# Attention's sums and outputs: 128-column weights split into two 64-column halves of the array

## The chip, the core and the metric

One core of a Trainium2 chip runs the whole kernel. The metric is the device time of one execution in microseconds. The engines that matter are TensorE (products into PSUM; the profile gives its products as PE and its weight loads as PEld), VectorE (DVE), ScalarE (ACT), GpSimd (POOL), and SyncE (SP), whose queue issues most transfers.

## The reference, cut to what matters

Four batches, eight heads, 576 positions, 64 columns a head; the attention is linear, without a softmax over positions:

```python
def phi(x):
    proj = np.einsum('bhsd,df->bhsf', x, w_phi)               # 128 features
    proj = proj - np.max(np.abs(proj), axis=-1, keepdims=True)
    return np.concatenate([np.exp(proj), np.exp(-proj)], axis=-1)
q_p, k_p = (phi(q), phi(k))
kv = np.einsum('bhsf,bhsd->bhfd', k_p, v)                     # the sums
z = np.sum(k_p, axis=2)
num = np.einsum('bhsf,bhfd->bhsd', q_p, kv)                   # the outputs
den = np.einsum('bhsf,bhf->bhs', q_p, z)[..., None] + 1e-06
attn = num / den
```

The result, 2304 x 512, goes through two MLPs (512 to 2048 to 512), the first with a leaky ReLU, the second with Mish. The MLP weights arrive as float64, everything else as float32; the result is float32.

## The kernel before, in words

The attention takes the 32 heads in 16 pairs of one batch, one pair a step; `attention(n)` is a step, and it is a software pipeline written out by hand: it loads pair n+3, transposes pair n+2 (`transposes`), projects pair n+1 (`q_proj`, `k_proj`), and makes the sums and outputs of pair n (`kv`, `kv_copy`, `nd`), while `x_t` brings the output of pair n-1 into the MLP's layout. All engines run their instructions in the order in which this code issues them.

Of a head's 576 positions 512 are four blocks of 128 (`NM` = 4); the last 64 (`LEFT`) of the two heads of a pair share a block of 128. For each sign `a` of the exponent, `kv(i, a)` multiplies `kp` as weights (128 positions x 128 features) with `vm` as the moving side: 64 columns of v and 64 columns of ones, so that the sum z comes out beside kv. One more product with `lp` and `vl` (2 x 65 columns) adds the left block. The sums of a pair fill one PSUM bank, `kv_copy` (L415, ACT) copies all 512 columns of it, and `nd` takes 128 columns of `qp` as weights with the 65 columns of `kv` that count, in two calls (c = 0, 1) of 16 profiled products each, c = 1 with the left block's 4 more. A product of two float32 operands appears in the profile as two weight loads and two products. VectorE then divides (L437 to L446).

Projections use operands split into two float32r parts, three products each (`three`, L80 to L82). `q_proj` products are copied by ACT (L389) into `qd`; after each second copy POOL reduces 128 partitions to their largest magnitude (L391), and `q_guard` (L396, DVE) subtracts it. `k_guard` (L351, L352, DVE) does the same for k along the free axis. In even pairs the left block of k of two pairs is projected as well, so such steps have one more pair of DVE instructions; in steps that transpose an even pair there is one more transposition and one more split.

Into the same steps, from step 1 on, the code weaves the conversion of the first MLP's float64 weights (`conv0`: `begin` before the transpositions, `join` between the two `nd` calls). In steps 1 to 10 `join` ends with a VectorE instruction (L149) and a ScalarE copy that waits for it (L202); in steps 11 to 15 the weight is stored by a DMA instead, and L202 is absent. After steps 8 to 11 a `window` splits a slice of the attention's result for the MLP (one more ACT copy and DVE subtraction). The next step's ACT copies of `qd` are queued behind these.

PSUM is used through two rings of four banks: "a" for projections and transpositions, "b" for the sums, the outputs and `x_t`.

Of the kernel before, what the change touches and what calls it, by code (L numbers as in the profile page):

```python
# [10 lines left out]
F32 = mybir.dt.float32  # L11
F32R = mybir.dt.float32r
AF = mybir.ActivationFunctionType
# [10 lines left out]
def attention_two_mlps_kernel(  # L24
# [12 lines left out]
    nc = tc.nc  # L37
    B, H, S, D = q.shape
# [3 lines left out]
    P = 128  # L42
    KD = DM // P
    M = DFF // P
    MAIN = 512
    NM = MAIN // P
    LEFT = S - MAIN
# [4 lines left out]
    HEAD = 2  # L52
    PAIRS = B * NP
    HM = MAIN // 2


    Q_COL = ((HM, 0, HM + P, P), (HM + LEFT, LEFT, HM + LEFT + P, LEFT + P))

# [8 lines left out]
    ap = tc.alloc_tile_pool(name="ap", bufs=2, reuse_waits="tile")  # L67
# [4 lines left out]
    def bank(ring):  # L72
        return ps.tile([P, 512], F32, tag=ring, name=ring)
# [15 lines left out]
    class Conv:  # L89
# [9 lines left out]
        def load(self, ahead):  # L99

            while self.loaded < min(self.at + ahead + 1, len(self.units)):
                u, kind = self.units[self.loaded]
                self.loaded += 1
                if kind == "fetch":
                    continue
                m, x = divmod(u, 2)
                stg = gp.tile([P, DM, 2], I32, tag="stage", name="stage")
                if x == 0:
                    src = w_in[self.which][:, m * P:(m + 1) * P].bitcast(I32).rearrange("(k p) f -> p k f", p=P)
                    dst = stg.rearrange("p (k f) t -> p k (f t)", k=KD)  # L110
                else:
                    src = w_out[self.which][m * P:(m + 1) * P, :].bitcast(I32)
                    dst = stg.rearrange("p f t -> p (f t)")
                nc.sync.dma_start(out=dst, in_=src)
                self.stage[u] = stg
# [122 lines left out]
    with tc.manual_schedule():  # L238
# [8 lines left out]
        nc.vector.memset(two, 2.0)  # L247

        NV = 3
        vmain = [ap.tile([P, 2, NM + 1, D], F32, name=f"vmain{i}", bufs=1) for i in range(NV)]  # L250

        vleft = [ap.tile([P, 2, D + 1], F32, name=f"vleft{i}", bufs=1) for i in range(NV)]
        for i in range(NV):
            nc.vector.memset(vmain[i][:, :, NM, :], 1.0)
            nc.vector.memset(vleft[i], 0.0)
            for r in range(2):
                nc.vector.memset(vleft[i][r * LEFT:(r + 1) * LEFT, r, D:D + 1], 1.0)
# [8 lines left out]
        def load(i):  # L266

            b, p = divmod(i, NP)
            h0 = 2 * p
            s = st[i]  # L270
            for nm, src in (("kn", k), ("qn", q)):
                s[nm] = ap.tile([P, 2, NM, D], F32, tag=nm, name=nm)
                for hs, eng in ([((0, 1), nc.sync), ((1, 2), nc.scalar)] if (i, nm) == (0, "kn") else [((0, 2), nc.sync)]):
                    hs = slice(*hs)
                    eng.dma_start(
                        out=s[nm][:, hs].rearrange("p h t d -> p h (t d)"),
                        in_=src[b, h0:h0 + 2, 0:MAIN, :][hs].rearrange("h (p t) d -> p h (t d)", t=NM),
                    )
                if (i, nm) == (0, "kn"):
                    for r in range(2):  # L280
                        nc.scalar.dma_start(out=wbd[r * D:(r + 1) * D, r, :], in_=w_phi)
            if i % 2 == 0:
                l = lf[i // 2]
                for nm, src, down, along in (("kl", k, 1, 2), ("ql", q, 2, 1)):
                    l[nm] = ap.tile([P, 2, D], F32, tag=nm, name=nm)
                    for r in range(2):
                        g0 = h0 + down * r
                        (nc.scalar if (i, nm) == (0, "ql") else nc.sync).dma_start(
                            out=l[nm][r * LEFT:(r + 1) * LEFT],
                            in_=src[b, g0:g0 + along + 1:along, MAIN:S, :].rearrange("h s d -> s h d"),  # L290
                        )

            def values():
                vm = s["vm"] = vmain[i % NV]
                nc.sync.dma_start(
                    out=vm[:, :, 0:NM, :].rearrange("p h t d -> p h (t d)"),
                    in_=v[b, h0:h0 + 2, 0:MAIN, :].rearrange("h (p t) d -> p h (t d)", t=NM),
                )
                vl = s["vl"] = vleft[i % NV]
                for r in range(2):  # L300
                    nc.sync.dma_start(out=vl[r * LEFT:(r + 1) * LEFT, r, 0:D], in_=v[b, h0 + r, MAIN:S, :])

            return values
# [12 lines left out]
        def transposes(i, *parts):  # L316
# [6 lines left out]
            for nm in parts or "kql":  # L323
                if nm != "l":
                    t = bank("a")
                    for j in range(NM):
                        nc.tensor.transpose(  # L327
                            out=t[:, j * P:(j + 1) * P],
                            in_=s[nm + "n"].rearrange("p h t d -> p (h t d)")[:, j * P:(j + 1) * P], identity=ident)
                    n = HM if nm == "k" else HM + LEFT  # L330
                    hi, lo = (ap.tile([P, 2, n], F32R, tag=f"{nm}t{x}", name=f"{nm}t{x}", bufs=1) for x in "hl")
                    s[nm + "h"], s[nm + "l"] = (x.rearrange("p h n -> p (h n)") for x in (hi, lo))
                    split(hi[:, :, 0:HM], lo[:, :, 0:HM], t.rearrange("p (h n) -> p h n", h=2))
                elif i % 2 == 0:
# [8 lines left out]
        def q_left(i):  # L343
            s, l = st[i], lf[i // 2]
            c = P + (i % 2) * LEFT
            for x in "hl":
                nc.vector.tensor_copy(out=s["q" + x][:, HM:HM + LEFT], in_=l[x][:, c:c + LEFT].bitcast(F32))

# [28 lines left out]
        def q_proj(i, c):  # L377
# [5 lines left out]
            t = bank("a")  # L383
            n = HM + (h == o) * LEFT
            c0 = h * (HM + (1 - o) * LEFT)
            d0 = (1 - o) * (HM + h * LEFT)
# [11 lines left out]
        def kv(i, a):  # L398

            s, l = st[i], lf[i // 2]  # L400
            if a == 0:
                s["kvp"] = bank("b")
            both = s["kvp"].rearrange("p (h a n) -> p h a n", h=2, a=2)

            for h in range(2):
                for t in range(NM):
                    nc.tensor.matmul(out=both[:, h, a, :], lhsT=s["kp"][a][:, h, t, :], rhs=s["vm"][:, h, t:NM + 1:NM - t, :],  # L407
                                     start=(a == 0 and h == 0 and t == 0), stop=False, skip_group_check=True)
            nc.tensor.matmul(out=both[:, :, a, 0:D + 1], lhsT=l["lp"][a][:, i % 2, :], rhs=s["vl"],  # L409
                             start=False, stop=(a == 1), skip_group_check=True)  # L410

        def kv_copy(i):
            s = st[i]
            s["kv"] = ap.tile([P, 4, P], F32, tag="kv", name="kv", bufs=1)
            nc.scalar.activation(out=s["kv"], in_=s["kvp"].rearrange("p (c n) -> p c n", n=P), func=AF.Copy)  # L415

        def nd(i, c):

            s = st[i]
            t = bank("b")  # L420
            ng = 4 + 2 * c
            g = t[:, 0:ng * (D + 1)].rearrange("p (c n) -> p c n", n=D + 1)
            if c == 0:
                s["xn"] = ap.tile([P, NM, 2, D], F32, tag="xn", name="xn")
            for j, u in enumerate(range(2 * c, 2 * c + 2)):
                for h in range(2):
                    for a in range(2):
                        nc.tensor.matmul(out=g[:, 2 * j + h], lhsT=s["qp"][a][:, h, Q_COL[h][u]:Q_COL[h][u] + P],  # L428
                                         rhs=s["kv"][:, 2 * h + a, 0:D + 1], start=(a == 0), stop=(a == 1))
            if c == 1:  # L430

                kv_ = s["kv"].rearrange("p (h a) n -> p h a n", a=2)
                for a in range(2):
                    nc.tensor.matmul(out=g[:, 4:6], lhsT=s["qp"][a].rearrange("p h n -> p (h n)")[:, MAIN:MAIN + P],  # L434
                                     rhs=kv_[:, :, a, 0:D + 1], start=(a == 0), stop=(a == 1))
            den = ap.tile([P, 6], F32, tag="den", name="den")[:, 0:ng]
            nc.vector.tensor_scalar(out=den, in0=g[:, :, D], scalar1=1e-6, scalar2=None, op0=ALU.add)  # L437
            nc.vector.reciprocal(out=den, in_=den)
            nc.vector.tensor_tensor(
                out=s["xn"][:, 2 * c:2 * c + 2].rearrange("p a h d -> p (a h) d"), in0=g[:, 0:4, 0:D],  # L440
                in1=den[:, 0:4].unsqueeze(2).to_broadcast([P, 4, D]), op=ALU.mult)
            if c == 1:
                s["xl"], s["lb"] = xleft[i % 2], t
                for h in range(2):
                    r = slice(h * LEFT, (h + 1) * LEFT)
                    nc.vector.tensor_scalar(out=s["xl"][r, h], in0=g[r, 4 + h, 0:D], scalar1=den[r, 4 + h:5 + h], scalar2=None,  # L446
                                            op0=ALU.mult)

        def x_t(i):
# [45 lines left out]
        def attention(n):  # L495
# [38 lines left out]
            if has_w:  # L534
                nd(w, 0)
# [252 lines left out]
```

## Time and profile before

| | |
|---|---|
| median of 3 runs | 1010.12 us (1010.07 to 1010.75) |
| the profiled execution | 1010.39 us |
| its span, first to last instruction | 1008.4 us |
| PE busy in the span | 1001.2 us, 99% |
| DVE busy, ACT busy | 732.4 us (73%), 500.8 us (50%) |
| `kv` and `nd` on the chain that ended last | L407 6%, L428 6%, L409 1%, L434 1% |

The attention takes about the first 220 us; the MLPs take the rest. The busy shares of the whole span say nothing about one stage, so the views below are cut to the attention's steps. The modelled end of a product's record lies after the start of the next, so the price of a product is read from the distance of starts, or from the chain of work, which counts no time twice.

### The profile page before, as it was taken

What the parts mean: (1) busy time and instruction counts of PE and PEld (TensorE: products, weight loads), DVE (VectorE), ACT (ScalarE), POOL (GpSimd) and SP (SyncE); (2) the same over time, 40 slices, a digit from 0 to 9 for tenths busy, and PEclk for the clock granted to TensorE, in tenths of its full rate; (3) what the DMA queues carried; (4) which work ended last, traced back from release to release, by engine and by line L of the source; (5) the groups of instructions that cost most, each with busy time, mean ns of one, the idle gap of its engine ahead of it and who ended that gap; (6) DMA issues with size and microseconds to landing.
All of it is one profiled execution on the core that took longest, in us unless ns stands there. A gap on an engine that the chain in (4) does not pass through costs nothing.

```text
span 1008.4 us, 14545 instructions
## 1 busy us (share of the span) xinstructions
PE 1001.2 (99%) x5552; PEld 874.8 (87%) x5552; DVE 732.4 (73%) x1366; ACT 500.8 (50%) x840; POOL 68.8 (7%) x36
## 2 busy tenths in 40 slices
PE   9999999999999999999999999999999999999998
PEld 8999999998888889988888888888888988888886
DVE  7788889749984566666435457978977888878875
ACT  6776777635553333333234445545544555445543
POOL 3333333300000000000000000000000000000000
PEclk9999999999999999999999999999999999999999
DMA  6233333224431444444301320000100100001001
GB/s 198 80 113 113 113 104 122 75 75 146 148 104 53 154 138 145 139 146 137 115 1 51 117 94 11 1 1 1 42 0 1 43 1 21 1 0 42 1 1 43
DMA packets 55654, 72.84 MB, mean 72 GB/s; under 512 B 10528, under 2 KB 40096, under 8 KB 55584
## 3 DMA queue, kind: packets, MB, share of 16 engines
q1 hardware_dynamic: 54848, 71.52, 22.0%
q8 instruction: 44, 0.72, 0.3%
q10 hardware_dynamic: 736, 0.39, 0.1%
q14 instruction: 26, 0.21, 0.1%
HBM read 57.48 MB, written 14.42 MB: 71 GB/s over the span
## 4 chain that ended last, share of the span: by engine, by line
PE 99%; DMA 1%; ACT 0%; ACTq 0%; DVE 0%; issue 0%
PE a L80 15%; PE a L81 15%; PE a L82 15%; PE b L80 13%; PE b L81 13%; PE b L82 13%; PE b L428 6%; PE b L407 6%; PE a L327 1%; PE b L434 1%; PE b L409 1%; PE b L454 1%; DMA ql<-in_q_dram 0%; PE b L457 0%; DMA kn<-in_k_dram 0%; PE a L337 0%
## 5 line engine op out<-in xcount | busy, mean ns | idle before, releaser
L80 PE MATMUL a<-wh,wh 128*128 128x512 f32 (+1 forms) x640 | 235.7, 368 | 0.0
L81 PE MATMUL a<-wl,wh 128*128 128x512 f32 (+1 forms) x640 | 235.4, 368 | 0.0
L82 PE MATMUL a<-wh,wl 128*128 128x512 f32 (+1 forms) x640 | 235.4, 368 | 0.0
L80 PEld LDWEIGHTS a<-wh,wh 128*128 128x128 f32 x640 | 120.7, 189 | 20.2
L81 PEld LDWEIGHTS a<-wl,wh 128*128 128x128 f32 x640 | 120.6, 189 | 20.1
L82 PEld LDWEIGHTS a<-wh,wl 128*128 128x128 f32 x640 | 120.7, 189 | 20.1
L636 DVE TENSOR_TENSOR gl<-g,gh 128x512 fp32r<-128x512 f32 x72 | 49.9, 693 | 110.4 <-ACT gh L633 110.4
L81 PE MATMUL b<-gl,wh 128*128 128x512 f32 (+1 forms) x320 | 117.7, 368 | 0.0
L80 PE MATMUL b<-gh,wh 128*128 128x512 f32 (+1 forms) x320 | 117.7, 368 | 0.0
L82 PE MATMUL b<-gh,wl 128*128 128x512 f32 (+1 forms) x320 | 117.7, 368 | 0.0
L80 PE MATMUL b<-wh,gh 128*128 128x512 f32 x288 | 112.1, 389 | 0.0
L81 PE MATMUL b<-wl,gh 128*128 128x512 f32 x288 | 112.1, 389 | 0.0
L82 PE MATMUL b<-wh,gl 128*128 128x512 f32 x288 | 112.0, 389 | 0.0
L633 ACT ACTIVATE gh<-g 128x512 fp32r<-128x512 f32 x72 | 45.5, 632 | 116.2 <-PE b L82 110.9
L658 ACT ACTIVATE gh<-u 128x512 fp32r<-128x512 f32 x72 | 45.5, 632 | 70.6 <-PE b L81 63.9
L391 POOL PARTITION_ALL_REDUCE qm<-qd x32 | 68.6, 2188 | 131.3 <-ACT qd L389 125.3
L632 DVE TENSOR_TENSOR g<-g,a 128x512 f32<-128x512 f32 x72 | 49.4, 686 | 38.5 <-ACT g L629 35.5
L685 ACT ACTIVATE r<-e,two 128x512 f32<-128x512 f32 x72 | 51.7, 718 | 36.3 <-DVE e L670 36.3
L82 PEld LDWEIGHTS b<-gh,wl 128*128 128x128 f32 x320 | 60.3, 189 | 10.0
L81 PEld LDWEIGHTS b<-gl,wh 128*128 128x128 f32 x320 | 60.4, 189 | 10.0
L80 PEld LDWEIGHTS b<-gh,wh 128*128 128x128 f32 x320 | 60.3, 188 | 9.9
L654 ACT ACTIVATE e<-a 128x512 f32<-128x512 f32 x72 | 43.0, 597 | 47.7 <-PE a L82 27.0
(116 smaller groups left out, 1757.5 us busy)
## 6 DMA issues: line engine op xcount, KB each, us to landing
stage<-in_moe_w_in_dram SPq DMA_DIRECT2D x32, 512.0 KB, 3.7
stage<-in_moe_w_out_dram SPq DMA_DIRECT2D x32, 512.0 KB, 3.5
scr<-c SPq DMA_DIRECT2D x37, 256.0 KB, 2.0
wstage<-scr SPq DMA_DIRECT2D x32, 256.0 KB, 3.9
qn<-in_q_dram SPq DMA_DIRECT2D x16, 256.0 KB, 4.3
vmain<-in_v_dram SPq DMA_DIRECT2D x16, 256.0 KB, 2.7
kn<-in_k_dram SPq DMA_DIRECT2D x15, 256.0 KB, 4.1
out_dram<-X SPq DMA_DIRECT2D x15, 256.0 KB, 2.2
```

Of the source, the lines that this page charges most:

```text
L80: nc.tensor.matmul(out=o, lhsT=wh_, rhs=xh, start=start, stop=False)
L81: nc.tensor.matmul(out=o, lhsT=wh_, rhs=xl, start=False, stop=False)
L82: nc.tensor.matmul(out=o, lhsT=wl_, rhs=xh, start=False, stop=stop)
L391: nc.gpsimd.partition_all_reduce(s["qm"][:, h, :], s["qd"][:, h, :], P, bass_isa.ReduceOp.absmax)
L407: nc.tensor.matmul(out=both[:, h, a, :], lhsT=s["kp"][a][:, h, t, :], rhs=s["vm"][:, h, t:NM + 1:NM - t, :], start=(a == 0 and h == 0 and ...
L428: nc.tensor.matmul(out=g[:, 2 * j + h], lhsT=s["qp"][a][:, h, Q_COL[h][u]:Q_COL[h][u] + P], rhs=s["kv"][:, 2 * h + a, 0:D + 1], start=(a = ...
L632: nc.vector.tensor_tensor(out=g, in0=g, in1=h, op=ALU.max)
L633: nc.scalar.activation(out=hi, in_=g, func=AF.Copy)
L636: nc.vector.tensor_tensor(out=lo, in0=g, in1=hi.bitcast(F32), op=ALU.subtract)
L654: nc.scalar.activation(out=e0, in_=h0, func=AF.Exp)
L658: nc.scalar.activation(out=hi2, in_=u2, func=AF.Copy)
L685: nc.scalar.activation(out=r0, in_=e0, func=AF.Ln, bias=two)
```

## The change

Each product with 128 columns of weights becomes two, one with weight columns 0 to 63, whose output goes to PSUM partitions 0 to 63, and one with columns 64 to 127 and partitions 64 to 127. The moving operand of both is the same. The ones of `vm` move next to v, one column for each block, so that 65 columns move instead of 128; v is then loaded by two transfers of a head each, into rows of 65. `kv_copy` copies 260 columns instead of 512. The left block of the outputs, so far 128 weights with 130 moving columns, becomes one product of 64 weights and 65 columns for each head; its denominators are 5 columns instead of 6.

```diff
+    HALVES = (slice(0, LEFT), slice(LEFT, 2 * LEFT))
...
-        vmain = [ap.tile([P, 2, NM + 1, D], F32, name=f"vmain{i}", bufs=1) for i in range(NV)]
+        vmain = [ap.tile([P, 2, NM, D + 1], F32, name=f"vmain{i}", bufs=1) for i in range(NV)]
...
-            nc.vector.memset(vmain[i][:, :, NM, :], 1.0)
+            nc.vector.memset(vmain[i][:, :, :, D:D + 1], 1.0)
...
-                nc.sync.dma_start(
-                    out=vm[:, :, 0:NM, :].rearrange("p h t d -> p h (t d)"),
-                    in_=v[b, h0:h0 + 2, 0:MAIN, :].rearrange("h (p t) d -> p h (t d)", t=NM),
-                )
+                for h in range(2):
+                    nc.sync.dma_start(out=vm[:, h, :, 0:D], in_=v[b, h0 + h, 0:MAIN, :].rearrange("(p t) d -> p t d", t=NM))
...
             for h in range(2):
                 for t in range(NM):
-                    nc.tensor.matmul(out=both[:, h, a, :], lhsT=s["kp"][a][:, h, t, :], rhs=s["vm"][:, h, t:NM + 1:NM - t, :],
-                                     start=(a == 0 and h == 0 and t == 0), stop=False, skip_group_check=True)
-            nc.tensor.matmul(out=both[:, :, a, 0:D + 1], lhsT=l["lp"][a][:, i % 2, :], rhs=s["vl"],
-                             start=False, stop=(a == 1), skip_group_check=True)
+                    for r in HALVES:
+                        nc.tensor.matmul(out=both[r, h, a, :], lhsT=s["kp"][a][:, h, t, r], rhs=s["vm"][:, h, t, :],
+                                         start=(a == 0 and h == 0 and t == 0), stop=False, skip_group_check=True)
+            for r in HALVES:
+                nc.tensor.matmul(out=both[r, :, a, :], lhsT=l["lp"][a][:, i % 2, r], rhs=s["vl"],
+                                 start=False, stop=(a == 1), skip_group_check=True)
...
-            s["kv"] = ap.tile([P, 4, P], F32, tag="kv", name="kv", bufs=1)
+            s["kv"] = ap.tile([P, 4, D + 1], F32, tag="kv", name="kv", bufs=1)
...
                     for a in range(2):
-                        nc.tensor.matmul(out=g[:, 2 * j + h], lhsT=s["qp"][a][:, h, Q_COL[h][u]:Q_COL[h][u] + P],
-                                         rhs=s["kv"][:, 2 * h + a, 0:D + 1], start=(a == 0), stop=(a == 1))
+                        for r in HALVES:
+                            nc.tensor.matmul(out=g[r, 2 * j + h], lhsT=s["qp"][a][:, h, q0 + r.start:q0 + r.stop],
+                                             rhs=s["kv"][:, 2 * h + a], start=(a == 0), stop=(a == 1))
             if c == 1:
...
                 for a in range(2):
-                    nc.tensor.matmul(out=g[:, 4:6], lhsT=s["qp"][a].rearrange("p h n -> p (h n)")[:, MAIN:MAIN + P],
-                                     rhs=kv_[:, :, a, 0:D + 1], start=(a == 0), stop=(a == 1))
+                    for h, r in enumerate(HALVES):
+                        nc.tensor.matmul(out=g[r, 4], lhsT=s["qp"][a].rearrange("p h n -> p (h n)")[:, MAIN + r.start:MAIN + r.stop],
+                                         rhs=s["kv"][:, 2 * h + a], start=(a == 0), stop=(a == 1))
```

## Rows read from the trace of the kernel before

**Rows 1.** The page: span and busy time (share, instructions) of each engine.

```profile
span 1008.4 us, 14545 instructions
...
PE 1001.2 (99%) x5552; PEld 874.8 (87%) x5552; DVE 732.4 (73%) x1366; ACT 500.8 (50%) x840; POOL 68.8 (7%) x36
```

**Rows 2.** Windows, one per step: length, busy us (instructions) of PE, PEld, DVE, ACT, POOL.

```profile
93.95:107.13 13.18, 13.18 (x117) 13.18 (x117) 10.76 (x26) 9.41 (x17) 4.91 (x3) 1.00 0.36 115
...
171.91:185.09 13.18, 13.18 (x117) 13.18 (x117) 11.01 (x26) 8.78 (x16) 4.62 (x3) 1.00 0.40 123
185.09:197.69 12.60, 12.60 (x112) 12.60 (x112) 10.05 (x24) 8.39 (x16) 3.91 (x3) 1.00 0.21 62
sum 167.96, PE 167.96 PEld 167.26 DVE 141.29 ACT 118.26 POOL 55.40; mean PE 12.92 PEld 12.87 DVE 10.87 ACT 9.10 POOL 4.26
```

**Rows 3.** The chain that ended last, in step 2: start us, us, work.

```profile
42.33 1.78 PE b L407 x16
...
46.35 0.87 PE a L327 x8
...
48.05 3.58 PE b L428 x32
51.62 0.50 PE b L434 x4
```

**Rows 4.** Timeline of PE: start us, us, line, out<-in, shapes, count.

```profile
95.57 0.39 PE L409 MATMUL b<-vleft,lp 128*128 128x130 f32 x2
95.79 1.95 PE L407 MATMUL b<-vmain,kp 128*128 128x128 f32 x16
...
151.31 0.22 PE L457 MATMUL b<-fold,xleft 128*128 128x64 f32 x1
...
151.37 0.28 PE L457 MATMUL b<-fold,xleft 128*128 128x64 f32 x1
```

**Rows 5.** Timelines of ACT, POOL and DVE around step 6 [idle before <-releaser].

```profile
91.24 0.63 ACT L202 ACTIVATE wh<-c 128x512 fp32r<-128x512 f32 x1 [2.01 <-DVE c L149]
91.78 1.30 ACT L389 ACTIVATE qd<-a 128x320 f32<-128x320 f32 x4
...
92.56 4.26 POOL L391 PARTITION_ALL_REDUCE qm<-qd  x2 [9.04 <-ACT qd L389]
...
96.19 1.06 ACT L374 ACTIVATE kp<-kd 128x1024 f32<-128x1024 f32 x1 [1.01 <-DVE kd L352]
...
96.86 1.36 DVE L396 TENSOR_TENSOR qd<-qd,qm 128x1152 f32<-128x1152 f32 x1 [0.78 <-POOL qm L391]
...
98.06 0.60 ACT L415 ACTIVATE kv<-b 128x512 f32<-128x512 f32 x1 [0.82 <-PE b L409]
...
103.03 0.69 DVE L149 SCALAR_TENSOR_TENSOR c<-c,e 128x512 int32<-128x512 int32 x1
...
103.75 0.63 ACT L202 ACTIVATE wh<-c 128x512 fp32r<-128x512 f32 x1 [1.89 <-DVE c L149]
```

**Rows 6.** Waits of DVE from 14 to 225 us: total us, times, longest.

```profile
DVE den L437 <- PE b L428: 6.5, 12, 1.9
```

**Rows 7.** Timelines of ACT and DVE, steps 13 to 15.

```profile
195.21 1.51 ACT L389 ACTIVATE qd<-a 128x320 f32<-128x320 f32 x4 [2.18 <-PE a L82]
...
213.28 0.60 ACT L415 ACTIVATE kv<-b 128x512 f32<-128x512 f32 x1 [2.02 <-PE b L409]
...
218.25 0.17 DVE L437 TENSOR_SCALAR den<-b 128x6 f32<-128x6 f32 x1
```

**Rows 8.** The chain's third piece, and the timeline of PE where it ends.

```profile
3.84 2.98 DMA ql<-in_q_dram
...
6.95 0.45 PE L337 MATMUL a<-ident,ql 128*128 128x128 f32 x1 [0.91 <-DMA ql<-in_q_dram]
```

**Rows 9.** The page's DMA issues: queue, count, KB each, us to landing.

```profile
vmain<-in_v_dram SPq DMA_DIRECT2D x16, 256.0 KB, 2.7
```

**Rows 10.** A window at the end of the kernel; columns as in rows 2, then PEclk.

```profile
1000.00:1008.40 8.40, 3.69 (x17) 2.73 (x15) 1.13 (x3) 1.58 (x3) 0.00 (x0) 0.85 0.35 126
```

More of the change, by code (lines that the diff above doesn't have):

```diff
@@ L402, in kv @@
                 s["kvp"] = bank("b")
-            both = s["kvp"].rearrange("p (h a n) -> p h a n", h=2, a=2)
+            both = s["kvp"][:, 0:4 * (D + 1)].rearrange("p (h a n) -> p h a n", h=2, a=2)
             for h in range(2):
                 for t in range(NM):
-                    nc.tensor.matmul(out=both[:, h, a, :], lhsT=s["kp"][a][:, h, t, :], rhs=s["vm"][:, h, t:NM + 1:NM - t, :],
-                                     start=(a == 0 and h == 0 and t == 0), stop=False, skip_group_check=True)
-            nc.tensor.matmul(out=both[:, :, a, 0:D + 1], lhsT=l["lp"][a][:, i % 2, :], rhs=s["vl"],
-                             start=False, stop=(a == 1), skip_group_check=True)
+                    for r in HALVES:
[4 more added lines that the diff above has]
+                                 start=False, stop=(a == 1), skip_group_check=True)
         def kv_copy(i):
             s = st[i]
-            s["kv"] = ap.tile([P, 4, P], F32, tag="kv", name="kv", bufs=1)
-            nc.scalar.activation(out=s["kv"], in_=s["kvp"].rearrange("p (c n) -> p c n", n=P), func=AF.Copy)
+            s["kv"] = ap.tile([P, 4, D + 1], F32, tag="kv", name="kv", bufs=1)
+            nc.scalar.activation(out=s["kv"], in_=s["kvp"][:, 0:4 * (D + 1)].rearrange("p (c n) -> p c n", n=D + 1), func=AF.Copy)
         def nd(i, c):
@@ L420, in nd @@
             t = bank("b")
-            ng = 4 + 2 * c
+            ng = 4 + c
             g = t[:, 0:ng * (D + 1)].rearrange("p (c n) -> p c n", n=D + 1)
@@ L426, in nd @@
                 for h in range(2):
+                    q0 = Q_COL[h][u]
                     for a in range(2):
-                        nc.tensor.matmul(out=g[:, 2 * j + h], lhsT=s["qp"][a][:, h, Q_COL[h][u]:Q_COL[h][u] + P],
-                                         rhs=s["kv"][:, 2 * h + a, 0:D + 1], start=(a == 0), stop=(a == 1))
+                        for r in HALVES:
+                            nc.tensor.matmul(out=g[r, 2 * j + h], lhsT=s["qp"][a][:, h, q0 + r.start:q0 + r.stop],
+                                             rhs=s["kv"][:, 2 * h + a], start=(a == 0), stop=(a == 1))
             if c == 1:
-                kv_ = s["kv"].rearrange("p (h a) n -> p h a n", a=2)
                 for a in range(2):
-                    nc.tensor.matmul(out=g[:, 4:6], lhsT=s["qp"][a].rearrange("p h n -> p (h n)")[:, MAIN:MAIN + P],
-                                     rhs=kv_[:, :, a, 0:D + 1], start=(a == 0), stop=(a == 1))
-            den = ap.tile([P, 6], F32, tag="den", name="den")[:, 0:ng]
+                    for h, r in enumerate(HALVES):
+                        nc.tensor.matmul(out=g[r, 4], lhsT=s["qp"][a].rearrange("p h n -> p (h n)")[:, MAIN + r.start:MAIN + r.stop],
+                                         rhs=s["kv"][:, 2 * h + a], start=(a == 0), stop=(a == 1))
+            den = ap.tile([P, 5], F32, tag="den", name="den")[:, 0:ng]
             nc.vector.tensor_scalar(out=den, in0=g[:, :, D], scalar1=1e-6, scalar2=None, op0=ALU.add)
@@ L443, in nd @@
                 s["xl"], s["lb"] = xleft[i % 2], t
-                for h in range(2):
-                    r = slice(h * LEFT, (h + 1) * LEFT)
-                    nc.vector.tensor_scalar(out=s["xl"][r, h], in0=g[r, 4 + h, 0:D], scalar1=den[r, 4 + h:5 + h], scalar2=None,
+                for h, r in enumerate(HALVES):
+                    nc.vector.tensor_scalar(out=s["xl"][r, h], in0=g[r, 4, 0:D], scalar1=den[r, 4:5], scalar2=None,
                                             op0=ALU.mult)
```

## The prediction

> **What bounds the kernel now.** I read the page first: PE is busy 99% of the span [rows 1]. That says only that nothing else ends last over the whole, so I cut windows at the start of `kv` in each step. In these thirteen windows PE has work all the time: 12.92 us a step on average, in practice 12.60 and 13.18 in turn. DVE has 10.87 of it, ACT 9.10, POOL 4.26 [rows 2]. So TensorE sets the step, but with only some 2 us to go before VectorE would.
>
> Then the price of a product, from the chain of work, which counts no time twice. 32 products of L428 take 3.58 us, 0.112 each, though only 65 columns move; 16 of L407 with 128 columns take 1.78, 0.111 each [rows 3]. The same price for half the columns: in `nd` it is not the moving side that costs. What a moving side costs is seen where 64 columns move: the two records of L457 start 0.06 us apart [rows 4]. So `nd` waits for its weights: a load of 128 columns paces it at 0.112, and a product of 65 columns would need 0.06. `kv` stands at both bounds at once. The left blocks cost the same: two of L409, with 130 columns, take 0.22 [rows 4], four of L434 0.50 with the step into the next line [rows 3]. Per step the change touches 36 products in `kv` and 36 in `nd`: 72 x 0.111 = 8.0 us, 62% of the step.
>
> Last, and this decides the size, what is queued on the other engines. In step 6 I followed the releasers: L202 on ACT starts the moment L149 on DVE is done; behind it in ACT's queue are the `qd` copies; two of them later POOL starts; 4.30 us after that `q_guard` starts on DVE, released by POOL; DVE then works without a pause of note down to L149, 6.17 us later; and L202 of the next step follows at 103.75 [rows 5]. That is a closed loop of 103.75 - 91.24 = 12.51 us a step in which the changed products appear only where DVE waits for `nd` before L437, 6.5 us in 12 places over the attention [rows 6].
>
> **The change, part by part.**
>
> *The products.* Twice as many, in pairs. Each half loads 64 columns, by half of the row 0.056, and moves 65, 0.06. If the halves of a pair overlap, a pair costs about 0.06; if they follow each other, 0.12. The trace has no product in half the array, so the bounds are: below, 0.058 for a pair; above, two full loads, 0.223 (a half load might cost a whole one). I take 0.06, because the two halves share neither columns of weights nor output partitions, and the nearest row, L457, is already there with one product. The left products of `kv` still move 130 columns, so a pair costs 0.11 overlapped. A step then has 68 x 0.06 + 4 x 0.11 = 4.5 us instead of 8.0: TensorE's work falls by 3.5 us to 9.1 and 9.7.
>
> *Changing between halves and the whole array.* Four times a step (into and out of `kv`, of `nd`). No row shows one. Below: nothing. Above: a product's record lasts 0.28 while starts are 0.11 apart, so waiting for the array to empty would cost 0.17, 0.7 us a step. It is covered as long as TensorE has slack in the step (next paragraph); without that cover it costs 16 x 0.7 = 11 us. The Trainium skill (TensorEngine Tiling (Array Packing), Key Properties) says both that tiles load and multiply in parallel, and that a change of tiling mode drains TensorE. By its first rule the sum stays as it is; its second alone, at the 0.17 above, speaks against the change and would take 11 us where TensorE has no slack, and nothing where it has. No run here shows either yet.
>
> *Where the 3.5 us a step go.* Three stretches, each with its own next bound.
> - Steps 2 to 10 contain L202, so the loop above holds. In steps that transpose a left block it is 12.51; in the others DVE has a split of 256 columns less, at L396's 1.36 for 1152 some 0.3, so 12.2, still above what DVE needs. Two steps cost 25.78 now and 24.7 then: 0.54 a step, 3.8 us over steps 2 to 8. In steps 9 and 10 the `window` copy, about 0.5 as L202's 91.24 to 91.78, is in the loop too, and nothing is left to gain. The condition is that `nd`'s first half is done when DVE comes to L437. `nd` waits for `kv_copy`, which stands in ACT's queue behind the exponential of `kd`; that ended at 97.25 [rows 5], so the copy, now half as long, could end by 97.7, sixteen pairs by 98.9, and DVE comes to L437, four instructions ahead of L149 (103.03), at about 101.4. It holds with more than 2 us to spare, so the pair's price hardly matters here. Steps 0 and 1 lack part of the loop; I give them 1.0 each.
> - Steps 11 to 13 have no L202, and `qd` waited for TensorE itself (2.18 us) [rows 7]. There DVE becomes the bound: 11.01 and 10.05 busy in windows of 13.18 and 12.60 [rows 2], with some 0.2 of gaps 2.0 and 2.4 saved; step 11 still has `window`'s subtraction, 1.0. Together 5.4.
> - Steps 14 and 15 have fewer transpositions and projections: ACT waits 2.02 us for `kv` and only then copies [rows 7]. From the start of step 14 to the end of `nd` (197.7 to 218.2) `kv` and `nd` take 16 us, of which 7 would go; the two exponentials ahead of the last `nd` on ACT, each about the 1.06 of [rows 5], hold back about 1. I take 6.2.
>
> Sum: 2.0 + 3.8 + 5.4 + 6.2 = 17.4 us out of the 56 that TensorE is relieved of. The MLPs behind it start that much earlier and are otherwise untouched, TensorE being busy throughout.
>
> *The loads of v.* One issue more a pair on SP's queue, and rows of 256 bytes instead of 1 KB. Landing takes 2.7 us now [rows 9], and a pair's v is issued three steps before its `kv`; even four times as long would be hidden behind more than two steps, 24 us. At the start there is no such cover: `ql` lands at 6.8 and TensorE waits 0.91 us for it [rows 8], and v's first loads share the engines with it. Between 0 and 1.5; I take 0.4, for a transfer that is on the path in part.
>
> *The rest.* `kv_copy` is about 0.25 shorter on ACT, off the path. The denominators and the ones columns change DVE by less than 0.1 us a step.
>
> The profiled execution took 1010.39 us (span 1008.4 and 2.0 around it), 0.3 above the median of the runs. 1010.4 - 17.4 + 0.4 = 993.
>
> **The rivals.**
> - *The halves follow each other.* If the weight path serves one load at a time, a pair costs 0.116 and the left ones 0.222: 68 x 0.116 + 4 x 0.222 = 8.8, so 0.8 a step more, 12 us; with the changes of mode up to 24. 1022 to 1034. For it: the loads pace these products today, and as many columns are loaded as before. Against: the halves are separate columns of the array. It decides from a pair price of 0.11 upward.
> - *Each half load costs a whole one.* Pair 0.223: 8.0 us a step more, about 1139. Against: nothing in the row says that a load has a fixed part that large, but no shorter load is there to see.
> - *Issue bounds.* A pair is now four instructions in 0.06 us; no stretch of the trace issues a load and a product more often than every 0.109 (L327, 0.87 for 8) [rows 3]. At 0.10 a pair TensorE keeps 12.5 of its 12.9 us and only the last steps gain: about 1004. It decides above 0.097 in steps 2 to 10 and above 0.075 later. The Trainium skill (TensorE: Matmul & The Clock Gate, Back-to-back issue gap) gives a floor of some 25 ns between starts; if loads counted like products, an estimate from that page is 0.10 a pair and the same 1004. By it, if only products counted, 993 stands.
> - *The clock.* With 2.6 to 3.2 us of slack a step TensorE pauses. In the last window PE is busy 3.69 of 8.40 us and the granted clock is 0.85 [rows 10], below full speed for part of it, so pauses can take the clock from 2.4 to 1.2 GHz. At half clock 9.4 us of work become 18.8, 6 us a step more, near 1090; it decides once more than 2.9 us of a step's work runs at the lower level. Against: granted 1.00 in the windows of the attention [rows 2], and the slack comes in pieces, some of it before `nd`, some before `k_proj`.
>
> **How the numbers follow.** Overlap 0.53, its own range 985 to 1001 (less if the early steps keep no gain or v's load costs its 1.5; more if DVE's waits shrink further). Issue bound 0.13, 1001 to 1010. Halves in sequence 0.25. Whole loads 0.05, clock 0.04. About 1008 to 1012 (within 0.2%, what a measurement of this kernel can tell from no change) I leave 0.06, from the dear end of the issue bound and the cheap end of the sequence; the rest of the latter is slower. So faster 0.64, same 0.06, slower 0.30. The range for 8 in 10 leaves out the whole loads, the clock, the dearest sequences and a little below: 985 to 1030.
>
> **What would show it.** PE busy of a step near 9.5 of some 12.4 in steps 2 to 10; waits of PE for ACT's `qd` copies and `kv_copy`, where there were none; L437 no longer waiting for L428; `q_guard` always released by POOL; 64 starts of L428's successor in under 2.2 us. If these take 3.7 or more, the overlap is wrong; if they take 2 and the steps stay at 12.9, the loop is longer than I read; if the steps fall below 12, it isn't closed.

## The result, and the profile after

The changed kernel takes 988.88 us (987.92 to 989.26, 4 runs) where the kernel before takes 1010.10: a ratio of 0.9788, 95% interval 0.9776 to 0.9800. The forecast was 993 in a range of 985 to 1030. The profiled execution took 988.86, its span 986.9.

The page's span and busy time, to hold against [rows 1]:

```profile
span 986.9 us, 16881 instructions
...
PE 957.1 (97%) x6704; PEld 819.9 (83%) x6704; DVE 728.2 (74%) x1366; ACT 494.9 (50%) x840; POOL 69.2 (7%) x36
```

TensorE is busy 44 us less and the span is 21.5 shorter: half of the relief has become waiting. Line numbers have moved: L81 to L83 are `three`, L326 the transpositions, L408 and L411 `kv`, L417 `kv_copy`, L433 and L439 `nd`, L388 the `qd` copies, L390 POOL, L350 and L351 `k_guard`, L395 `q_guard`, L373 the exponentials, L150 `join`, L203 the copy that waits for it, L442 the denominators. The timeline of PE in step 6 (start us, us, line, tiles, shapes, count) shows the price of a pair:

```profile
87.81 0.28 PE L83 MATMUL a<-wbh,ktl 128*128 128x256 f32 x1
88.02 1.15 PE L408 MATMUL b<-vmain,kp 128*64 128x65 f32 x32
89.00 0.39 PE L411 MATMUL b<-vleft,lp 128*64 128x130 f32 x4
89.22 1.10 PE L408 MATMUL b<-vmain,kp 128*64 128x65 f32 x32
90.16 0.39 PE L411 MATMUL b<-vleft,lp 128*64 128x130 f32 x4
90.48 0.66 PE L326 MATMUL a<-ident,kn 128*128 128x128 f32 x4
...
92.33 2.09 PE L433 MATMUL b<-kv,qp 128*64 128x65 f32 x64
94.24 0.40 PE L439 MATMUL b<-kv,qp 128*64 128x65 f32 x8
```

64 records of L433, 32 pairs, start within 94.24 - 92.33 = 1.91 us: 0.060 a pair, where one product of 128 columns took 0.112 [rows 3]. Two pairs of L411 take 0.22. `kv` now lasts 2.5 us instead of 4.0. Windows of one step's length, columns as in [rows 2]:

```profile
88.70:101.00 12.30, 10.08 (x182) 9.34 (x179) 10.31 (x25) 8.57 (x16) 4.26 (x3) 1.00 0.37 105
...
125.80:138.30 12.50, 10.33 (x184) 9.42 (x182) 11.44 (x28) 9.35 (x18) 4.30 (x3) 0.95 0.44 121
...
151.10:161.58 10.48, 10.26 (x204) 9.55 (x202) 10.06 (x25) 8.77 (x17) 4.33 (x4) 1.00 0.31 70
161.58:172.40 10.82, 10.07 (x189) 9.52 (x186) 10.41 (x25) 8.33 (x15) 4.77 (x3) 1.00 0.52 150
```

Two regimes are to be seen: steps of 12.3 us in which neither TensorE nor VectorE is full, and, without L203, steps of 10.5 to 10.8 in which both nearly are (VectorE 96%, TensorE 98 and 93%). What holds the long ones together is read from the timelines of ACT, POOL and DVE, which answer to [rows 5]:

```profile
85.39 0.63 ACT L203 ACTIVATE wh<-c 128x512 fp32r<-128x512 f32 x1 [1.71 <-DVE c L150]
85.92 1.29 ACT L388 ACTIVATE qd<-a 128x320 f32<-128x320 f32 x4
...
86.71 4.27 POOL L390 PARTITION_ALL_REDUCE qm<-qd  x2 [8.04 <-ACT qd L388]
...
91.01 1.36 DVE L395 TENSOR_TENSOR qd<-qd,qm 128x1152 f32<-128x1152 f32 x1 [0.79 <-POOL qm L390]
...
96.97 0.69 DVE L150 SCALAR_TENSOR_TENSOR c<-c,e 128x512 int32<-128x512 int32 x1
...
97.70 0.63 ACT L203 ACTIVATE wh<-c 128x512 fp32r<-128x512 f32 x1 [2.30 <-DVE c L150]
```

The same links as before, 12.31 us round (12.51 then). TensorE, which waited for nothing in these steps, now waits in the loop's shadow, and VectorE waits for `nd` only once more, in step 15; the waits of PE over the span, then of DVE from 14 to 210 us (total us, times, longest):

```profile
PE a L81 <- ACT qd L388: 15.3, 10, 2.0
PE b L433 <- ACT kv L417: 3.3, 8, 1.2
...
DVE qd L395 <- POOL qm L390: 4.4, 6, 0.9
...
DVE den L442 <- PE b L433: 0.6, 1, 0.6
```

Where the time came from is counted at POOL's starts, one pair of reductions a step. The timeline of POOL in the kernel before, the starts of steps 2, 9, 11 and 14:

```profile
40.65 4.26 POOL L391 PARTITION_ALL_REDUCE qm<-qd  x2 [8.70 <-ACT qd L389]
...
131.37 4.38 POOL L391 PARTITION_ALL_REDUCE qm<-qd  x2 [9.05 <-ACT qd L389]
...
157.57 4.38 POOL L391 PARTITION_ALL_REDUCE qm<-qd  x2 [8.66 <-ACT qd L389]
...
196.01 4.26 POOL L391 PARTITION_ALL_REDUCE qm<-qd  x2 [8.69 <-ACT qd L389]
```

and in the changed kernel:

```profile
37.84 4.26 POOL L390 PARTITION_ALL_REDUCE qm<-qd  x2 [7.70 <-ACT qd L388]
...
123.79 4.26 POOL L390 PARTITION_ALL_REDUCE qm<-qd  x2 [8.56 <-ACT qd L388]
...
149.07 4.26 POOL L390 PARTITION_ALL_REDUCE qm<-qd  x2 [8.56 <-ACT qd L388]
...
181.04 4.47 POOL L390 PARTITION_ALL_REDUCE qm<-qd  x2 [6.42 <-ACT qd L388]
```

The differences grow from 2.81 (steps 0 and 1) to 7.58 (4.77 in steps 2 to 8), 8.50 (0.92 in steps 9 and 10) and 14.97 (6.47 in steps 11 to 13). The MLP's first product behind the last `nd` starts at 197.07 instead of 217.97, 20.9 earlier (5.93 in steps 14 and 15); the last 0.6 lies in the MLPs.

### The profile page after: what moved, and what is told of

It is laid out like the page before. It is cut to its first block, busy times and chain, and to the rows that moved or that the text cites. A ratio compares the mean times of both kernels' runs of the same rounds, so it can differ in the third digit from the quotient of the medians.

```text
span 986.9 us, 16881 instructions
## 1 busy us (share of the span) xinstructions
PE 957.1 (97%) x6704; PEld 819.9 (83%) x6704; DVE 728.2 (74%) x1366; ACT 494.9 (50%) x840; POOL 69.2 (7%) x36
## 4 chain that ended last, share of the span: by engine, by line
PE 84%; DVE 9%; POOL 3%; ACT 1%; issue 1%; DMA 1%; ACTq 0%; DVEq 0%
PE a L81 14%; PE a L83 14%; PE a L82 14%; PE b L81 13%; PE b L82 13%; PE b L83 13%; POOL qm L390 3%; DVE qd L395 2%; DVE ktl L78 1%; DVE qtl L78 1%; PE b L408 1%; DVE c L150 1%; DVE e L147 1%; ACT qd L388 1%; DVE wl L204 1%
## 5 line engine op out<-in xcount | busy, mean ns | idle before, releaser
L81 PE MATMUL a<-wh,wh 128*128 128x512 f32 (+1 forms) x640 | 235.9, 369 | 0.0
L83 PE MATMUL a<-wh,wl 128*128 128x512 f32 (+1 forms) x640 | 235.7, 368 | 0.0
L81 PEld LDWEIGHTS a<-wh,wh 128*128 128x128 f32 x640 | 120.7, 189 | 20.4 <-issue 0.2
L83 PEld LDWEIGHTS a<-wh,wl 128*128 128x128 f32 x640 | 120.7, 189 | 20.1
L81 PE MATMUL b<-gh,wh 128*128 128x512 f32 (+1 forms) x320 | 117.8, 368 | 0.0
L83 PE MATMUL b<-gh,wl 128*128 128x512 f32 (+1 forms) x320 | 117.8, 368 | 0.0
L81 PE MATMUL b<-wh,gh 128*128 128x512 f32 x288 | 112.2, 390 | 0.0
L83 PE MATMUL b<-wh,gl 128*128 128x512 f32 x288 | 112.2, 389 | 0.0
L390 POOL PARTITION_ALL_REDUCE qm<-qd x32 | 69.0, 2203 | 116.1 <-ACT qd L388 116.1
L83 PEld LDWEIGHTS b<-gh,wl 128*128 128x128 f32 x320 | 60.4, 189 | 10.0
L81 PEld LDWEIGHTS b<-gh,wh 128*128 128x128 f32 x320 | 60.4, 189 | 10.0
```

Of the source, the lines that this page charges most:

```text
L81: nc.tensor.matmul(out=o, lhsT=wh_, rhs=xh, start=start, stop=False)
L83: nc.tensor.matmul(out=o, lhsT=wl_, rhs=xh, start=False, stop=stop)
L390: nc.gpsimd.partition_all_reduce(s["qm"][:, h, :], s["qd"][:, h, :], P, bass_isa.ReduceOp.absmax)
```

## The experiments

My theory: the two halves of the array load and multiply side by side; that takes 3.5 us a step off TensorE; and in steps 2 to 10 most of it is lost to the loop through L203, `qd`, POOL and VectorE. The rivals: shorter loads or fewer moving columns do it, without any overlap; and the time saved goes with the time taken off TensorE, without a loop.

**The halves not next to each other (e1_not_adjacent).** The same products, all of one half first:

```diff
-            for h in range(2):
-                for t in range(NM):
-                    for r in HALVES:
+            for r in HALVES:
+                for h in range(2):
+                    for t in range(NM):
...
-            for j, u in enumerate(range(2 * c, 2 * c + 2)):
-                for h in range(2):
-                    q0 = Q_COL[h][u]
-                    for a in range(2):
-                        for r in HALVES:
+            for r in HALVES:
+                for j, u in enumerate(range(2 * c, 2 * c + 2)):
+                    for h in range(2):
+                        q0 = Q_COL[h][u]
+                        for a in range(2):
```

> The changed kernel with its products in another order: all products of one half of the array first, then all of the other (in the sums 16 starts of one half in a row and the left products still in pairs, in the outputs 16 in a row), the same loads, the same products. Theory (two halves overlap, and what is bought is that overlap): neighbours in the queue now use the same half and follow each other, 0.058 us each, 0.116 for two, so the sums and outputs cost at least the 8.0 us a step of the kernel before and TensorE sets the step again: 1010 to 1025 us. Rival (shorter loads and fewer moving columns are what is bought, the halves need not overlap): 989 us, as the changed kernel. A queue that looks far enough ahead to start the other half early would give a time between.

Measured: 1004.53 us (ratio to before 0.9946, 0.9931 to 0.9961), between the two forecasts. Nearly three quarters of the gain are gone with the order alone, so the overlap of neighbours is most of what is bought. It is not all gone, and the timeline of PE says why:

```profile
92.00 1.73 PE L408 MATMUL b<-vmain,kp 128*64 128x65 f32 x29
93.51 0.33 PE L411 MATMUL b<-vleft,lp 128*64 128x130 f32 x1
93.56 0.28 PE L408 MATMUL b<-vmain,kp 128*64 128x65 f32 x2
```

29 starts take 93.51 - 92.00 = 1.51 us, 0.052 each, against 0.031 (32 in 0.98) when halves alternate. Within one half the trace has starts 0.055 to 0.061 apart, half of the 0.112 that 128 columns of weights take; only where the code passes to the other half do three pairs of starts lie 2 to 6 ns apart. After L411 has begun, products of L408, which the code issues first, still start: the engine looks a little ahead, and between the halves its starts do not keep the order of issue that the description of the kernel gives for all engines. `kv` takes 3.8 us here (92.00 to 95.79) and `nd` 3.6 (97.63 to 101.21), each less than the 4.0 of full width, which is why the forecast of no gain was too dear.

**One part alone (e2_kv_alone, e3_nd_alone).** In the first, `nd` has its 128 columns of weights and the left block's product back; in the second, `kv`:

```diff
-                        for r in HALVES:
-                            nc.tensor.matmul(out=g[r, 2 * j + h], lhsT=s["qp"][a][:, h, q0 + r.start:q0 + r.stop],
-                                             rhs=s["kv"][:, 2 * h + a], start=(a == 0), stop=(a == 1))
+                        nc.tensor.matmul(out=g[:, 2 * j + h], lhsT=s["qp"][a][:, h, q0:q0 + P],
+                                         rhs=s["kv"][:, 2 * h + a], start=(a == 0), stop=(a == 1))
...
```

```diff
-                    for r in HALVES:
-                        nc.tensor.matmul(out=both[r, h, a, :], lhsT=s["kp"][a][:, h, t, r], rhs=s["vm"][:, h, t, :],
-                                         start=(a == 0 and h == 0 and t == 0), stop=False, skip_group_check=True)
+                    nc.tensor.matmul(out=both[:, h, a, :], lhsT=s["kp"][a][:, h, t, :], rhs=s["vm"][:, h, t, :],
+                                     start=(a == 0 and h == 0 and t == 0), stop=False, skip_group_check=True)
...
```

> Halves in the sums alone, the outputs as before (128 columns of weights), layout as in the changed kernel. Theory (a loop through ACT, POOL and DVE bounds steps 2 to 10 at 12 to 12.3 us, so that half of TensorE's relief is enough there): TensorE needs some 11 us a step, steps 2 to 10 keep their whole gain, the last steps lose some 5 us of theirs: 994 us, 16 of the 21 us with half the relief. Rival (the gain goes with the time taken off TensorE): half of it, 999 to 1000 us.

> Halves in the outputs alone, the sums with 128 columns of weights and 65 moving. Theory (the loop bounds steps 2 to 10): 994 to 996 us, so that the gains of the two parts alone add up to some 30 us, more than the 21 of both. Rival (gain in proportion to TensorE's time): 999 to 1000 us, adding up to 21.

Measured: 995.25 (0.9851, 0.9834 to 0.9867) and 994.10 (0.9841, 0.9827 to 0.9856). Either half of the relief brings 15 to 16 us, together 31, and both at once 21. In each, POOL's starts of steps 2 and 9 lie as far apart as in the changed kernel (85.98 and 86.27 us, against 85.95), first in e2_kv_alone, then in e3_nd_alone:

```profile
38.52 4.26 POOL L390 PARTITION_ALL_REDUCE qm<-qd  x2 [7.76 <-ACT qd L388]
...
124.50 4.26 POOL L390 PARTITION_ALL_REDUCE qm<-qd  x2 [8.57 <-ACT qd L388]
```

```profile
38.55 4.26 POOL L390 PARTITION_ALL_REDUCE qm<-qd  x2 [8.07 <-ACT qd L388]
...
124.82 4.26 POOL L390 PARTITION_ALL_REDUCE qm<-qd  x2 [8.56 <-ACT qd L388]
```

0.7 us of what each loses lies ahead of step 2, most of the rest behind the start of step 11. So in steps 2 to 8 more relief buys nothing, as the loop says, and the rival by which the gain goes with TensorE's time (999 to 1000 us) falls.

**All but the halves (e4_layout_alone).** 128 columns of weights in both parts, and the new layout, loads and copy:

> No halves at all: 128 columns of weights throughout, but all else of the change (65 moving columns in the sums instead of 128, v loaded in rows of 256 bytes, the copy of 260 columns instead of 512). Theory (weight loads pace these products at 0.112 us whatever moves): 1010 us, within 1. Rival (the moving columns paced the sums): a product of the sums at 0.06, 1.7 us a step less, about 996 us.

Measured: 1009.27 (0.9989, 0.9979 to 0.9998), some 1 us. The chain of work in that run:

```profile
40.41 1.73 PE b L407 x16
...
46.13 3.57 PE b L430 x32
```

16 products of `kv` with 65 moving columns take 1.73, 0.108 each, against 1.78 with 128 [rows 3]: half the moving columns are worth 0.003 us a product. With e1_not_adjacent, where 64 columns of weights cost half of that, it is the columns of weights that pace a product and not a fixed price of each.

**The loop cut, in both kernels (e5_loop_cut, e6_loop_cut_before).** L203 is issued one step later, behind the `qd` copies and the exponentials of q:

```diff
...
-                self.rest = split_w(self.which, u // 2, u % 2, c)
+                self.late = lambda: split_w(self.which, u // 2, u % 2, c)
...
                 st[w]["qp"] = [exp(st[w]["qd"], "qp", sg) for sg in (1, -1)]
+            if conv0.late is not None:
+                conv0.rest, conv0.late = conv0.late(), None
```

> The changed kernel with one ScalarE instruction moved: the copy behind the weight conversion (the one that waits for VectorE's join and stands ahead of the next step's copies of the q projections) is issued one step later, behind those copies and the exponentials of q, where ScalarE has idle time. Same work. Theory (in steps 2 to 10 the loop of 12 to 12.3 us through that copy, POOL and VectorE is what ends last): the loop is open, VectorE with some 10.8 to 11 us a step becomes the bound, 1.1 us a step less over nine steps: 977 to 981 us. Rival (the loop is only what the trace happens to show, and TensorE's own waits or VectorE bound the step): 988 to 989 us, no change.

> The same move in the kernel before, with its 128 columns of weights. Theory (TensorE sets the steps there, except where a window copy stretches the loop): 1009 to 1010 us, at most 1 us less. Rival (the loop bounded the kernel before as well, and TensorE's 99% only hid it): 3 us less or more, 1007 us or below.

Measured: 978.23 in the changed kernel (0.9685, 0.9670 to 0.9699), 10.7 us below it; 1009.97 in the kernel before (0.9999, 0.9989 to 1.0008). The same edit is worth 1% behind the change and nothing ahead of it: the loop binds only once TensorE does not. Windows of two steps, the timeline of ACT, and the waits of PE and DVE from 14 to 200 us in e5_loop_cut:

```profile
58.03:68.76 10.73, 9.90 (x186) 9.35 (x185) 10.24 (x25) 8.61 (x16) 4.67 (x2) 1.00 0.44 128
68.76:79.95 11.19, 10.00 (x187) 9.48 (x186) 10.58 (x25) 8.84 (x17) 4.77 (x3) 1.00 0.49 133
```

```profile
67.96 1.50 ACT L388 ACTIVATE qd<-a 128x320 f32<-128x320 f32 x4 [0.64 <-PE a L83]
69.36 2.21 ACT L373 ACTIVATE qp<-qd 128x1152 f32<-128x1152 f32 x2
71.46 0.62 ACT L203 ACTIVATE wh<-c 128x512 fp32r<-128x512 f32 x1
```

```profile
PE b L433 <- ACT kv L417: 11.6, 12, 1.8
...
DVE qd L395 <- POOL qm L390: 0.6, 2, 0.4
```

The `qd` copies start at 67.96, before L150 of that step (68.71), POOL is done before VectorE needs it, VectorE is busy 95% of the step, and TensorE waits mostly in front of `nd`. That VectorE alone is the next bound, as expected above, is not shown: its work leaves little room, but the chain of work from 37 to 113 us lies on TensorE for 42%, on VectorE for 24 and on ScalarE for 22. This version beats both kernels.

## Why the prediction was right, step by step

**The pair.** 0.06 forecast, 0.060 measured; left pairs 0.11 and 0.11. Two rivals fall with it. Halves in sequence: only e1's order makes them so. Issue: four instructions go out in 0.060 us. The Trainium skill (TensorE: Matmul & The Clock Gate, Back-to-back issue gap) gives a floor of some 25 ns between starts. Between the two halves of a pair it is not kept: most start 5 to 8 ns apart, though on the mean a start comes every 30 ns; the measurement decides. The issue rival's 12.5 us and 0.097 come out only with some 0.35 us for the changes of mode, which its text does not name; without them they are 12.2 and 0.103, and at 0.060 nothing hangs on it.

**The changes of mode** (between halves and the whole array). Bounded at 0.17 and left uncosted under TensorE's slack. The rows show them: L408 starts 0.21 after the last projection product where such products step by 0.12, and the first transposition starts 0.32 after the last four records of L411 began, where they take 0.22; in each case the next start is some 0.05 late as well. In the kernel before, the same two places take 0.12 (93.67 to 93.79) and 0.22 (97.58 to 97.80). So 0.15 a change; at four a step, an estimate of 0.6 us of TensorE. The Trainium skill (TensorEngine Tiling (Array Packing), Key Properties) says that such a change drains the engine, and that tiles work in parallel. The trace agrees with the second by the pair's 0.060 and with the first by the 0.15, but that it is the draining that costs it is not shown. The cover was there in steps 2 to 10: from 38 to 111 us TensorE has 4% of the chain of work. It was not there in steps 11 to 13, where it has 65% (153 to 183 us). The 0.6 on top of the forecast's 9.1 and 9.7 us a step gives 9.7 and 10.3; PE is busy 10.1 to 10.3 in the steps of the loop, where the sign to look for was 9.5.

**Where the relief goes.** Forecast 2.0, 3.8, 0, 5.4 and 6.2 us for steps 0 and 1, 2 to 8, 9 and 10, 11 to 13, 14 and 15; measured 2.8, 4.8, 0.9, 6.5 and 5.9. Four terms were a little small, hence 993 for 989. For steps 0 and 1 the 1.0 each was a guess without a row, and 0.6 of the 2.8 is there already when POOL starts in step 0 (16.86 instead of 17.48). The loop of steps 2 to 10 holds; it runs in 12.31 and 11.95 instead of 12.5 and 12.2, because VectorE's stretch in it, 6.17 us before, still held short waits for TensorE (91.01 to 96.97 now, 5.96); that also left something in steps 9 and 10, where I saw nothing. Steps below 12 were to show that the loop is not closed; at 11.95 that sign was drawn too tight, and e5_loop_cut shows the loop. In steps 11 to 13 the size came out near, but VectorE as the bound is only half of it: it is busy 93 to 96% of them, while most of the chain lies on TensorE, and with half of the relief (e2_kv_alone) these steps take 11.7 to 12.0 us instead of 10.4 to 11.2. Of the three it is step 11 that I sized too small: from POOL's start at 149.07 to the next at 159.48 are 10.4 us, before from 157.57 to 170.24 12.7, so 2.3 us where I gave 1.0.

**A detail that was wrong.** I said that POOL would always release `q_guard`. It did in 6 places. In steps that project a left block of k, VectorE's own queue ends later; the chain of work in one of them:

```profile
74.09 0.39 PE a L81
...
75.11 0.70 DVE mx L350
...
78.71 1.34 DVE qd L395
```

There the loop runs from the first `qd` copy, which frees the PSUM bank for `k_proj`, over TensorE and `k_guard`, as long as POOL's way.

**The loads of v.** I charged 0.4 at the start; nothing came. The last `ql` landed at 6.60 (issued at 4.07, 2.53 on the chain) instead of 6.82 [rows 8], and TensorE waited 0.9 for it as before.

**The clock.** It did fall once within the steps of the profiled run, for some 3 us of one step, which is some 1.7 us of work at full clock; the rival, with a chance of 0.04, wanted more than 2.9 us of a step's work there. See below.

## What to carry to other kernels

Here a float32 product of 128 columns of weights costs 0.11 us whether 65 or 128 columns move: its weights pace it. Two halves of the array work side by side, so splitting the weights and alternating the halves in the queue nearly doubles the rate (0.112 to 0.060 us), while the order half by half gives most of that away. Before counting such relief in full, follow the releasers once round a step on the other engines: a copy that waits for one engine and stands ahead of the next step's work in an in-order queue closes a loop that no busy share shows. When a change brings half of what it frees, look for that loop first; moving one instruction here brought another 1%.

## What the runs showed of the hardware that was not expected

The clock fell in step 10 of the profiled run of the changed kernel and cost nothing. Windows of 2 us (columns as in [rows 10]), then PE's timeline:

```profile
136.00:138.00 2.00, 2.00 (x14) 1.78 (x14) 1.36 (x3) 2.00 (x5) 1.75 (x1) 0.76 1.07 374
138.00:140.00 2.00, 2.00 (x37) 2.00 (x38) 1.66 (x3) 0.87 (x1) 2.00 (x2) 0.50 0.04 14
140.00:142.00 2.00, 2.00 (x44) 1.82 (x41) 1.45 (x2) 1.32 (x2) 0.52 (x1) 0.89 0.04 8
```

```profile
135.94 0.39 PE L81 MATMUL a<-wbh,kth 128*128 128x256 f32 x1 [1.95 <-ACT qd L388]
136.16 0.28 PE L82 MATMUL a<-wbl,kth 128*128 128x256 f32 x1
136.28 0.28 PE L83 MATMUL a<-wbh,ktl 128*128 128x256 f32 x1
...
137.17 0.42 PE L81 MATMUL a<-wbh,kth 128*128 128x256 f32 x1
137.38 0.42 PE L82 MATMUL a<-wbl,kth 128*128 128x256 f32 x1
```

TensorE had waited 1.95 us for the `qd` copies; about a microsecond after it resumed, a product of 256 columns takes 0.21 instead of 0.12, and the granted clock is 0.50, 1.2 GHz, until some way into the third window. The length of the pause alone does not decide: a step earlier TensorE had waited longer, and no fall followed, nor did one after pauses of 1.79 and 1.45 us in steps 6 and 7:

```profile
123.47 0.39 PE L81 MATMUL a<-wbh,kth 128*128 128x256 f32 x1 [1.97 <-ACT qd L388]
```

Step 10 still took 12.82 us (POOL from 136.25 to 149.07), as did step 8, which also ends with a `window`, at full clock (110.97 to 123.79). In e2_kv_alone, at a granted clock of 1.00, step 10 took 12.83. No piece of the chain of work between 125 and 150 us lies on TensorE: half clock for some 3 us fits into its slack. In e5_loop_cut, with pauses of up to 1.84 us, the clock was 1.000 over the span.
